# Values of three batches as one split fp32r product, exponentials in mid-batch, scores spaced out

## The chip, the cores and the metric

The kernel runs on one core of one Trainium2 chip. The metric is device microseconds for one execution. The core has five engines with queues of their own: TensorE (PE; PEld is its weight load), VectorE (DVE), ScalarE (ACT), GpSimd (POOL) and SyncE (SP), which here issues every DMA. An instruction waits on semaphores, and what stands behind it on its engine waits with it.

## The reference

Four batches of 12480 tokens with 128 channels go through an attention over 49 agents, and then through a feed-forward network with cosine.

```python
def sm(a, b):                                   # softmax of scaled scores
    s = scale * (a @ b.transpose(0, 2, 1))
    s = s - s.max(-1, keepdims=True)
    e = np.exp(s)
    return e / (e.sum(-1, keepdims=True) + 1e-09)
agent_v = sm(agents, k) @ v                     # per batch: 49 x 128
x = sm(q, agents) @ agent_v                     # 12480 x 128
h = x @ w_in                                    # 128 -> 2048
out = (h * np.cos(h)) @ w_out                   # 2048 -> 128
```

## The kernel before, in words

A batch is cut into 13 groups of 960 tokens, and a group into 8 tiles of 120 tokens. There are two kinds of work.

The main loop (lines 500 to 535) turns weights of the queries into output. It has 832 steps: 4 batches x 13 groups x 16. A step takes two 128-wide slices of the hidden layer and 480 tokens: two matmuls into `ph` (L507; the left side is `a`, which is the agents' values already multiplied by `w_in`, the right side is `pT`), a sine with a quarter-turn of bias on ACT (L510), `(cos - 1) * h` on DVE (L512), and four steps later two matmuls with `w_out` into `one` (L528). The missing `h @ w_out` is added by two matmuls with `b1`, `b2` (L523, L524) at the start of each 480 tokens. Every 8 steps ACT copies `one` to `osb` (L530). `ph` has three buffers in PSUM; `one` has two, and everything else that needs PSUM shares them.

All other work is put between the steps by a plan. `plan(n, f)` runs f behind step n; `extra(n, f)` looks for the next free step of which (n - 4) mod 8 is 1, 3 or 5, so that at most three such pieces stand in 8 steps. A tile scheduler then orders each engine's queue, with this program order as priority, so a piece can come out a few steps earlier or later. The pieces are:

- scores of keys (`scores`, L85): 8 fp32 matmuls, which the hardware profile shows as 16; ACT copies the result to `s` (L163) and DVE keeps a running maximum (L174). `top`, `across` and `spread` make the maximum of all 12480 keys, and `shift` (L202) subtracts it, on POOL in three lots.
- scores of queries (`query`, L85 too): 8 fp32 matmuls, then a maximum and a subtraction on DVE (L334, L341).
- a burst of exponentials: ACT loads another table, runs three exponentials of keys (L206) and those of a set of queries (L345, `pieces`), and loads the table of the sine again. `query_sums` follows on DVE (L349 to L351).
- values (`values`, L224): per group one DMA of v (`vt`, four buffers), 8 fp32 matmuls of 98 columns (the 49 weights twice), shown as 16, and an addition into `av` on DVE (L229). POOL adds up the exponentials for the denominator (`add`, L214); `total` and `inverse` sum them across and take the reciprocal.
- `project` (L255 to L263): four matmuls with `w_in` make the next batch's `a`; `project_out` makes `b1`, `b2`.
- for every group of queries `query_weights` on POOL (L355), `query_turned`: transposes on PE (L364), a copy on ACT (L366), and two casts and two subtractions on POOL (L369, L370) that split the weights into two fp32r parts in `pT`. They are planned 10 and 7 steps ahead of the group's first step.

During batch b's steps the plan prepares batch b + 1: in the order scores of keys, `shift`, scores of queries, burst, values, projection, each as early as `extra` allows. Batch 0 is prepared ahead of the loop, with its values summed in PSUM (`wide`); its own queries 3 to 12 are done in the loop's first 40 steps, with two short bursts.

Of the kernel before, what the change touches and what calls it, by code (L numbers as in the profile page):

```python
# [18 lines left out]
P = 128  # L19
TT = 120  # L20
GT = 8
HT = GT // 2
# [3 lines left out]
EPS = 1e-9  # L26
# [8 lines left out]
HI = 64  # L35
# [5 lines left out]
def agent_attention_cos_ffn(ctx, tc, qT, kT, v, agT, w_in, w_out, outT):  # L41
    nc = tc.nc
    NB, _, N = qT.shape
    NA = agT.shape[2]
    KR = HI + NA
# [6 lines left out]
    NG = N // GRP  # L52
# [8 lines left out]
    make_identity(nc, ident)  # L61
    ones = const.tile([P, 1], F32, name="ones")
    nc.gpsimd.memset(ones, 1.0)
    half_pi = const.tile([P, 1], F32, name="half_pi")
# [32 lines left out]
    class Weights:  # L97
# [45 lines left out]
    class Agents:  # L143
# [72 lines left out]
        def values(self, g):  # L216
            vt = self.sb.tile([TT, GT, P], F32, name="vt", bufs=4)
            nc.sync.dma_start(vt, v[self.b, :, g * GT:(g + 1) * GT, :])
            lone = self.wide is not None
            if g == 0 or not lone:  # L220
                self.po = self.copies(self.wide()[:, 0] if lone else self.psum())
            e, po = self.part(g), self.po
            for t in range(GT):
                nc.tensor.matmul(po, vt[:, t, :], twice(e[:, t, :]), start=(t == 0 and (g == 0 or not lone)),  # L224
                                 stop=(t == GT - 1 and (g == NG - 1 or not lone)))
            if g == (NG - 1 if lone else 0):
                nc.vector.tensor_copy(self.sums, po)
            elif not lone:
                nc.vector.tensor_add(self.sums, self.sums, po)  # L229
# [8 lines left out]
        def inverse(self):  # L238

            pa = self.psum()  # L240
            nc.tensor.matmul(pa[:KR, :1], self.es2, ones[:TT], start=True, stop=True)
            z = self.sb.tile([KR, 1], F32, name="z", bufs=1)
            nc.vector.tensor_scalar_add(z, pa[:KR, :1], EPS)
# [47 lines left out]
    with ExitStack() as pools:  # L291
        sb = pools.enter_context(tc.tile_pool(name="sb", bufs=2))
# [25 lines left out]
        STEP = NCH * NP  # L318
        PER = NG * STEP
        NQ = NB * NG  # L320
        NSTEP = NB * PER
# [59 lines left out]
        if NG == 13:  # L381
            pieces0 = [(0, 1, 2), (3, 4, 5, 6, 7), (8, 9, 10, 11, 12)]
            pieces1 = [(0, 1, 2, 3), (4, 5, 6, 7), (8, 9, 10, 11, 12)]
        pieces = [[tuple(b * NG + g for g in piece) for piece in (pieces1 if b else pieces0)] for b in range(NB)]
        lots = [(0, 4), (4, 4), (8, 5)]


        pre = Plan()
# [4 lines left out]
            pre(3 * c + 2, ws.w_in, c)  # L393
        pre(NG, ab[0].top)
        pre(NG, ab[0].across)
        for n in pieces[0][0]:
            pre(NG, query, n, pieces[0][0], True)
        pre(NG, ab[0].spread)
        for j, (g, n) in enumerate(lots):
            for k in range(g, g + n):  # L400
# [4 lines left out]
        end = 2 * NG + 4  # L405
# [14 lines left out]
        pre(end - 2, query_exp, pieces[0][0])  # L420
        pre(end - 1, query_sums, pieces[0][0])
        pre(end - 1, query_weights, 0)
        pre(end, sine_table)
        pre(end, query_turned, 0)
# [14 lines left out]
        def extra(n, f, *args):  # L439


            while n in taken or (n - LAG) % NP not in (1, 3, 5):
                n += 1
            taken.add(n)
            plan(n, f, *args)
            return n
# [2 lines left out]
            plan(n * STEP - 10, query_weights, n)  # L449
            extra(n * STEP - 7, query_turned, n)  # L450

        def burst(n, todo):
            for f, args in todo:
                plan(n, f, *args)

        t = 0
        for piece in pieces[0][1:]:
            for n in piece:
                t = extra(t, query, n, piece) + 1
            t += 2  # L460
            assert t < piece[0] * STEP - 10
            plan(t, query_exp, piece)
            plan(t + 1, query_sums, piece)
            if piece is pieces[0][1]:
                first = t
        for b in range(1, NB):
            o = (b - 1) * PER
            t = o + (24 if b == 1 else 0)
            for g in range(NG):
                t = extra(t, ab[b].scores, g) + 1  # L470
            t += 2
            plan(t, ab[b].top)
            t = extra(t + 1, ab[b].across)
            t = extra(t + 2, ab[b].spread) + 1
            for g, n in lots:
                plan(t, ab[b].shift, g, n, nc.gpsimd)
            for piece in pieces[b]:
                for n in piece:
                    t = extra(t, query, n, piece) + 1
            t += 2  # L480
            for g, n in lots:
                plan(t, pinned_exp, ab[b], g, n)
            for piece in pieces[b]:
                plan(t, query_exp, piece)
                plan(t + 1, query_sums, piece)
# [10 lines left out]
            assert t < o + PER - 4, (t, o + PER)  # L496


        rs = {}
# [175 lines left out]
```

## Time and profile before

| | |
|---|---|
| median of 3 runs | 1282.7 us (1281.45 to 1284.28) |
| the profiled execution | 1278.94 us, of it 1277.2 us from the first to the last instruction |
| busy: PE, DVE, ACT, POOL | 93%, 85%, 79%, 25% of the span |
| granted TensorE clock | 0.982 on average |

Busy shares are means over stages with different limits. Matmuls overlap, so PE's share says little about how near PE is to its peak; the distance between the starts of two matmuls in the timeline says more. A row of a view with stretches gives the length of a stretch and the busy time of an engine in it.

### The profile page before, as it was taken

What the parts mean: (1) busy time and instruction counts of PE and PEld (TensorE: products, weight loads), DVE (VectorE), ACT (ScalarE), POOL (GpSimd) and SP (SyncE); (2) the same over time, 40 slices, a digit from 0 to 9 for tenths busy, and PEclk for the clock granted to TensorE, in tenths of its full rate; (3) what the DMA queues carried; (4) which work ended last, traced back from release to release, by engine and by line L of the source; (5) the groups of instructions that cost most, each with busy time, mean ns of one, the idle gap of its engine ahead of it and who ended that gap; (6) DMA issues with size and microseconds to landing.
All of it is one profiled execution on the core that took longest, in us unless ns stands there. A gap on an engine that the chain in (4) does not pass through costs nothing.

```text
span 1277.2 us, 17186 instructions
## 1 busy us (share of the span) xinstructions
PE 1186.0 (93%) x6349; PEld 948.7 (74%) x6349; DVE 1087.8 (85%) x1214; ACT 1010.1 (79%) x1115; POOL 313.6 (25%) x341
## 2 busy tenths in 40 slices
PE   8889999996999999969999999997999999999996
PEld 8867787775987887759866787876986666666664
DVE  6878888787789788877899888887789999999997
ACT  2358888667689887677799888667789999999996
POOL 1012113315122124151232223215222212221220
PEclk9999999997999999989999999997999999999999
DMA  9952342332431432414300233322400000000000
GB/s 319 253 165 82 120 125 78 94 108 62 126 91 39 130 96 80 130 55 133 100 32 16 78 109 93 120 67 62 109 16 32 31 32 16 32 31 32 16 32 34
DMA packets 31016, 107.72 MB, mean 84 GB/s; under 512 B 3436, under 2 KB 3820, under 8 KB 30924
## 3 DMA queue, kind: packets, MB, share of 16 engines
q1 hardware_dynamic: 30924, 106.54, 27.2%
q8 instruction: 52, 0.85, 0.3%
q14 instruction: 40, 0.33, 0.1%
HBM read 80.97 MB, written 25.56 MB: 83 GB/s over the span
## 4 chain that ended last, share of the span: by engine, by line
PE 66%; DVE 13%; ACT 12%; issue 5%; DMA 2%; POOL 1%; ACTq 0%; SPq 0%; POOLq 0%; DVEq 0%
PE ph L507 24%; PE one L528 16%; PE one L85 11%; DVE r L512 10%; PE one L224 6%; ACT c L510 6%; ACT osb L530 3%; PE one L523 3%; PE one L364 2%; PE one L524 1%; DMA vt<-v 1%; DVE mx L334 1%; PE ph L93 1%; ACT e L345 1%; PE ph L224 1%
## 5 line engine op out<-in xcount | busy, mean ns | idle before, releaser
L510 ACT ACTIVATE c<-ph,half_pi 128x960 f32<-128x960 f32 x832 | 864.7, 1067 | 194.4 <-PE ph L507 181.1
L512 DVE SCALAR_TENSOR_TENSOR r<-c,ph 128x960 fp32r<-128x960 f32 x832 | 926.1, 1149 | 107.0 <-ACT c L510 97.0
L507 PE MATMUL ph<-pT,a 113*128 113x480 f32 x1664 | 539.4, 405 | 25.0 <-DVE r L512 21.7
L528 PE MATMUL one<-r,w 128*128 128x480 f32 x1664 | 514.5, 389 | 0.7 <-DVE r L512 0.7
L507 PEld LDWEIGHTS ph<-pT,a 113*128 113x128 f32 x1664 | 285.8, 190 | 149.5 <-DVE r L512 89.3
L528 PEld LDWEIGHTS one<-r,w 128*128 128x128 f32 x1664 | 308.8, 190 | 45.7 <-DVE r L512 1.9
L355 POOL TENSOR_TENSOR p<-e,rz 120x392 f32<-120x392 f32 x52 | 44.1, 849 | 779.5 <-PE one L364 677.1
L85 PEld LDWEIGHTS one<-ag,xt 128*120 128x120 f32 x1408 | 165.3, 184 | 19.2 <-ACT osb L530 11.0
L85 PE MATMUL one<-ag,xt 128*120 128x49 f32 x1408 | 163.8, 264 | 2.6 <-ACT osb L530 1.7
L370 POOL TENSOR_TENSOR pT<-p,pT 49x480 fp32r<-49x480 f32 x104 | 126.8, 1219 | 8.0
L224 PE MATMUL one<-s,vt 120*128 120x98 f32 x624 | 81.3, 285 | 26.6 <-ACT osb L530 26.6
L224 PEld LDWEIGHTS one<-s,vt 120*128 120x128 f32 x624 | 81.6, 205 | 30.3 <-ACT osb L530 27.9
L369 POOL CAST pT<-p 49x480 fp32r<-49x480 f32 x104 | 61.1, 587 | 57.2 <-ACT p L366 52.3
L530 ACT COPY osb<-one 128x480 f32<-128x480 f32 x104 | 57.9, 557 | 2.1 <-PE one L528 2.1
L523 PE MATMUL one<-pT,b 113*128 113x480 f32 x104 | 46.1, 443 | 12.0 <-ACT osb L530 6.7
L334 DVE TENSOR_REDUCE mx<-one 120x8 f32<-120x392 f32 x49 | 27.6, 563 | 29.0 <-PE one L85 28.9
L523 PEld LDWEIGHTS one<-pT,b 113*128 113x128 f32 x104 | 19.5, 187 | 35.5 <-issue 12.5
L364 PE MATMUL one<-ident,p 120*113 120x120 f32 x208 | 37.2, 279 | 5.4 <-ACT s L163 1.8
L364 PEld LDWEIGHTS one<-ident,p 120*113 120x113 f32 x208 | 28.4, 176 | 18.3 <-ACT osb L530 11.3
L524 PE MATMUL one<-pT,b 113*128 113x480 f32 x104 | 39.6, 381 | 0.0
L202 POOL TENSOR_TENSOR s<-s,mxb 120x1568 f32<-120x1568 f32 (+1 forms) x9 | 31.4, 3518 | 27.2 <-DVE mxb L198 27.2
L349 DVE TENSOR_REDUCE rz<-e 120x32 f32<-120x1568 f32 (+2 forms) x12 | 22.7, 1916 | 17.2 <-ACT e L345 17.2
(91 smaller groups left out, 506.2 us busy)
## 6 DMA issues: line engine op xcount, KB each, us to landing
xt<-qT SPq DMA_DIRECT2D x52, 480.0 KB, 3.4
vt<-v SPq DMA_DIRECT2D x52, 480.0 KB, 4.3
outT<-osb SPq DMA_DIRECT2D x51, 480.0 KB, 2.5
xt<-kT SPq DMA_DIRECT2D x46, 480.0 KB, 3.4
c<-kT SPq DMA_DIRECT2D x6, 480.0 KB, 6.1
raw<-w_in SPq DMA_DIRECT2D x4, 512.0 KB, 6.1
raw<-w_out SPq DMA_DIRECT2D x4, 512.0 KB, 10.2
outT<-osb SPq DMA_DIRECT2D x2, 240.0 KB, 2.0
```

The source lines that it names most:

```text
L85: nc.tensor.matmul(ps[:, t, :], xt[:, t * TT:(t + 1) * TT], ag[:, b, :], start=True, stop=True)
L224: nc.tensor.matmul(po, vt[:, t, :], twice(e[:, t, :]), start=(t == 0 and (g == 0 or not lone)), stop=(t == GT - 1 and (g == NG - 1 or not ...
L364: nc.tensor.transpose(pt[:KR, t * TT:(t + 1) * TT], p_in[n % 2][:, t, :KR], ident[:TT, :TT])
L369: nc.gpsimd.tensor_copy(pT[own, c], p[own])
L370: nc.gpsimd.tensor_sub(pT[other, c], p[own], pT[own, c].bitcast(F32))
L507: nc.tensor.matmul(ph[:, j, :CH], ai[:, f], pTs[q % 3][:, c], start=True, stop=True)
L510: nc.scalar.activation(cos, h, AF.Sin, bias=half_pi, scale=1.0)
L512: nc.vector.scalar_tensor_tensor(r, cos, 1.0, h, op0=ALU.subtract, op1=ALU.mult)
L523: nc.tensor.matmul(po, b1[k], pTs[q % 3][:, c], start=True, stop=False)
L524: nc.tensor.matmul(po, b2[k], pTs[q % 3][:, c], start=False, stop=False)
L528: nc.tensor.matmul(po, w1[:, f, :], r[:, j, :], start=False, stop=(f == NF - 1))
L530: nc.scalar.copy(osb[:, c * CH:(c + 1) * CH], po)
```

## The change

For batches 1 to 3 the values are made another way. GpSimd rounds each v tile to fp32r and takes the remainder, so that the two parts and two columns of ones stand side by side in `v12` (258 columns); it does the same with the exponentials in `e12` (98 columns). One fp32r matmul for each tile multiplies all parts with all parts, and the columns of ones give the denominators. This is done in two halves of four tiles, each with two buffers (`v12` shares those of `raw`). DVE adds the 98 x 258 result up in `o`. `folded` adds the parts together with three small matmuls by a constant matrix `fold`, and replaces `total` and `inverse`; `add` is no longer called in these batches.

The plan changes too. Queries are scored in other sets: 3 to 7 at the start, then 8 to 19 during batch 0, 20 to 32 during batch 1, 33 to 45 during batch 2, and 46 to 51 during batch 3. Scores of keys and queries alternate, and `spread_out` spaces them. The burst has a fixed place: behind step 112 of batch 0, and behind step 98 of the others. The values follow it, one group in five steps at the earliest. Ahead of the burst stand `top`, `across`, `spread` and `shift`. There is one short burst less at the start and one more in batch 3.

```diff
+    fold = const.tile([2 * NA, KR], F32, name="fold")     # + memset and four affine_selects on gpsimd
...
-            raw = self.sb.tile([P, 512, 2], U32, name="raw", bufs=2)
+            raw = self.sb.tile([P, 516, 2], U32, name="raw", bufs=2)[:, :512]
...
     class Fast(Agents):
+        def values(self, g):
+            if self.wide is not None:
+                return super().values(g)
+            sb = self.sb
+            W = 2 * P + 2
+            vt = sb.tile([TT, GT, P], F32, name="vt", bufs=4)
+            nc.sync.dma_start(vt, v[self.b, :, g * GT:(g + 1) * GT, :])
+            if g == 0:
+                self.o = sb.tile([2 * NA, W], F32, name="o", bufs=1)
+            e, po = self.part(g), self.psum()[:2 * NA, :W]
+            for h in range(2):
+                ts = slice(h * HT, (h + 1) * HT)
+                v12 = sb.tile([TT, HT, W], F32R, name="raw", bufs=2)
+                e12 = sb.tile([TT, HT, 2 * NA], F32R, name="e12", bufs=2)
+                nc.gpsimd.memset(v12[:, :, 2 * P:].bitcast(F32), 1.0)
+                for x12, x, w in ((v12, vt[:, ts, :], P), (e12, e[:, ts, :], NA)):
+                    nc.gpsimd.tensor_copy(x12[:, :, :w], x)
+                    nc.gpsimd.tensor_sub(x12[:, :, w:2 * w], x, x12[:, :, :w].bitcast(F32))
+                for t in range(HT):
+                    nc.tensor.matmul(po, e12[:, t], v12[:, t], start=(h == t == 0), stop=(h == 1 and t == HT - 1))
+            if g == 0:
+                nc.vector.tensor_copy(self.o, po)
+            else:
+                nc.vector.tensor_add(self.o, self.o, po)
+
+        def folded(self):
+            pa = self.psum()
+            for x in range(2):
+                nc.tensor.matmul(pa[:, :KR], self.o[:, x * P:(x + 1) * P], fold, start=(x == 0), stop=(x == 1))
+            nc.tensor.matmul(pa[:KR, 256:257], fold, self.o[:, 2 * P:2 * P + 1], start=True, stop=True)
+            nc.vector.tensor_copy(self.av, pa[:, :KR])
+            self.inverse_of(pa[:KR, 256:257])
...
+        BURST = [112] + [98] * (NB - 1)
+        early = [(3, 4, 5, 6, 7)]
+        pieces, n = [], 8
+        for b in range(1, NB + 1):
+            upto = min(b * NG + 7, NQ)
+            k = upto - n
+            cuts = [n + k * i // 3 for i in range(4)]
+            pieces.append([tuple(range(x, y)) for x, y in zip(cuts, cuts[1:]) if y > x])
+            n = upto
...
+        def spread_out(todo, t, end):
+            for i, lot in enumerate(todo):
+                t = extra(t, *lot) + 1
+                if i + 1 < len(todo):
+                    t += max(0, (end - t) // (len(todo) - i - 1) - 1)
+            return t
+        def burst(t, end, group):
+            for piece in group:
+                plan(t, query_exp, piece)
+                plan(t + 1, query_sums, piece)
...
         for b in range(1, NB):
             o = (b - 1) * PER
-            t = o + (24 if b == 1 else 0)
-            for g in range(NG):
-                t = extra(t, ab[b].scores, g) + 1
-            t += 2
+            at = o + BURST[b - 1]
+            both = ...                       # scores of keys and of queries, alternating
+            last = spread_out(both, t, at - 18)
+            t = last + 1
             plan(t, ab[b].top)
             t = extra(t + 1, ab[b].across)
             t = extra(t + 2, ab[b].spread) + 1
             for g, n in lots:
                 plan(t, ab[b].shift, g, n, nc.gpsimd)
-            for piece in pieces[b]:
-                for n in piece:
-                    t = extra(t, query, n, piece) + 1
-            t += 2
             for g, n in lots:
-                plan(t, pinned_exp, ab[b], g, n)
-            for piece in pieces[b]:
-                plan(t, query_exp, piece)
-                plan(t + 1, query_sums, piece)
+                plan(at, pinned_exp, ab[b], g, n)
+            burst(at, o + PER, group)
+            t = at + 1
             for g in range(NG):
-                plan(t, ab[b].add, g)
-                t = extra(t, ab[b].values, g) + 1
-            plan(t, ab[b].total)
-            t = extra(t + 1, ab[b].inverse) + 1
+                t = max(extra(t, ab[b].values, g) + 1, at + 1 + 5 * (g + 1))
+            t = extra(t + 1, ab[b].folded) + 1
...
+        at = (NB - 1) * PER + BURST[NB - 1]
+        assert spread_out(scored(pieces[NB - 1]), t, at - 4) < at
+        burst(at, NSTEP, pieces[NB - 1])
```

More of the change, by code (lines that the diff above doesn't have):

```diff
@@ L61, in agent_attention_cos_ffn @@
     make_identity(nc, ident)
+    fold = const.tile([2 * NA, KR], F32, name="fold")
+    nc.gpsimd.memset(fold, 0.0)
+    for part in (fold[:, :NA], fold[:, HI:]):
+        for base in (0, -NA):
+            nc.gpsimd.affine_select(out=part, in_=part, compare_op=ALU.not_equal, fill=1.0,
+                                    base=base, pattern=[[-1, NA]], channel_multiplier=1)
     ones = const.tile([P, 1], F32, name="ones")
@@ L241, in inverse, with inverse_of @@
             nc.tensor.matmul(pa[:KR, :1], self.es2, ones[:TT], start=True, stop=True)
+            self.inverse_of(pa[:KR, :1])
+        def inverse_of(self, sums):
             z = self.sb.tile([KR, 1], F32, name="z", bufs=1)
-            nc.vector.tensor_scalar_add(z, pa[:KR, :1], EPS)
+            nc.vector.tensor_scalar_add(z, sums, EPS)
             self.rz = self.sb.tile([KR, 1], F32, name="rz", bufs=1)
@@ L380, in agent_attention_cos_ffn @@
         ab = [Fast(sb, small, b, None if b else pair) for b in range(NB)]
[L381 to L384, printed above, removed]
+        assert NG == 13
+        BURST = [112] + [98] * (NB - 1)
[7 more added lines that the diff above has]
+            n = upto
         lots = [(0, 4), (4, 4), (8, 5)]
+        first = (0, 1, 2)
         pre = Plan()
@@ L395, in agent_attention_cos_ffn @@
         pre(NG, ab[0].across)
-        for n in pieces[0][0]:
-            pre(NG, query, n, pieces[0][0], True)
+        for n in first:
+            pre(NG, query, n, first, True)
         pre(NG, ab[0].spread)
@@ L419, in agent_attention_cos_ffn @@
             pre(NG + 5 + 3 * c, w_product, c)
-        pre(end - 2, query_exp, pieces[0][0])
-        pre(end - 1, query_sums, pieces[0][0])
+        pre(end - 2, query_exp, first)
+        pre(end - 1, query_sums, first)
         pre(end - 1, query_weights, 0)
@@ L450, in agent_attention_cos_ffn, with scored @@
             extra(n * STEP - 7, query_turned, n)
[L452 to L457, printed above, removed]
-            for n in piece:
-                t = extra(t, query, n, piece) + 1
-            t += 2
-            assert t < piece[0] * STEP - 10
-            plan(t, query_exp, piece)
-            plan(t + 1, query_sums, piece)
-            if piece is pieces[0][1]:
-                first = t
+        def spread_out(todo, t, end):
[6 more added lines that the diff above has]
+            for piece in group:
+                assert t + 4 < piece[0] * STEP - 2 and t < end
+                plan(t, query_exp, piece)
+                plan(t + 1, query_sums, piece)
+        def scored(group):
+            return [(query, n, piece) for piece in group for n in piece]
+        t = spread_out(scored(early), 0, 0) + 2
+        burst(t, 3 * STEP, [early[0]])
         for b in range(1, NB):
             o = (b - 1) * PER
-            t = o + (24 if b == 1 else 0)
-            for g in range(NG):
-                t = extra(t, ab[b].scores, g) + 1
-            t += 2
+            at = o + BURST[b - 1]
+            group = pieces[b - 1]
+            qs, ks = scored(group), [(ab[b].scores, g) for g in range(NG)]
+            both = []
+            while qs or ks:
+                both += ks[:1] + qs[:1]
+                ks, qs = ks[1:], qs[1:]
+            last = spread_out(both, t, at - 18)
+            t = last + 1
             plan(t, ab[b].top)
@@ L476, in agent_attention_cos_ffn @@
                 plan(t, ab[b].shift, g, n, nc.gpsimd)
-            for piece in pieces[b]:
-                for n in piece:
-                    t = extra(t, query, n, piece) + 1
-            t += 2
+            assert t <= at, (t, at)
             for g, n in lots:
-                plan(t, pinned_exp, ab[b], g, n)
-            for piece in pieces[b]:
-                plan(t, query_exp, piece)
-                plan(t + 1, query_sums, piece)
+                plan(at, pinned_exp, ab[b], g, n)
+            burst(at, o + PER, group)
+            t = at + 1
             for g in range(NG):
-                plan(t, ab[b].add, g)
-                t = extra(t, ab[b].values, g) + 1
-            plan(t, ab[b].total)
-            t = extra(t + 1, ab[b].inverse) + 1
+                t = max(extra(t, ab[b].values, g) + 1, at + 1 + 5 * (g + 1))
+            t = extra(t + 1, ab[b].folded) + 1
             i = b % 2
@@ L495, in agent_attention_cos_ffn @@
             plan(t, ab[b].judge)
-            assert t < o + PER - 4, (t, o + PER)
+            t += 1
+            assert t < o + PER - 3, (t, o + PER)
+        at = (NB - 1) * PER + BURST[NB - 1]
+        assert spread_out(scored(pieces[NB - 1]), t, at - 4) < at
+        burst(at, NSTEP, pieces[NB - 1])
         rs = {}
```

## The prediction

> **What bounds the kernel now.** First the page's busy shares.
>
> ```profile
> span 1277.2 us, 17186 instructions
> PE 1186.0 (93%) x6349; PEld 948.7 (74%) x6349; DVE 1087.8 (85%) x1214; ACT 1010.1 (79%) x1115; POOL 313.6 (25%) x341
> ```
>
> Three engines are near their limit and POOL has room, on average. A mean hides stages, so second the stretches: the four periods of 208 steps, with DVE's L512, one for each step.
>
> ```profile
> core 0: us, DVE busy (x), PEclk, DMA share, GB/s
> 81.10:410.20 329.10, 231.80 (x207) 0.98 0.31 94
> 410.20:718.50 308.30, 231.28 (x207) 0.98 0.27 82
> 718.50:1026.60 308.10, 231.15 (x207) 0.98 0.24 72
> 1026.60:1268.00 241.40, 231.84 (x212) 1.00 0.07 28
> ```
>
> Third, the same view of the second period's stages, and the steps of the last one that have nothing beside them.
>
> ```profile
> 410.20:471.30 61.10, 45.39 (x40) 1.00 0.38 117
> 471.30:481.50 10.20, 8.95 (x9) 1.00 0.07 28
> 481.50:548.30 66.80, 45.11 (x41) 1.00 0.37 111
> 548.30:573.40 25.10, 7.85 (x7) 0.80 0.15 40
> 573.40:632.50 59.10, 44.35 (x41) 1.00 0.44 126
> 632.50:653.40 20.90, 17.81 (x17) 1.00 0.06 24
> 653.40:708.60 55.20, 52.92 (x49) 1.00 0.07 27
> 708.60:718.50 9.90, 8.89 (x8) 1.00 0.07 10
> 1026.60:1246.90 220.30, 211.25 (x193) 1.00 0.07 28
> ```
>
> The bare step is 220.3 / 192 = 1.148 us, and DVE is busy 211.25 of 220.3 us there: DVE sets it. 208 steps make 238.8 us, so the periods cost 90.3, 69.5, 69.3 and 2.6 us above the floor, 231.7 in all. A change can only win from these. By stage (the cuts lie at steps 0, 40, 48, 88, 96, 136, 152, 200): scores of keys 61.1 - 45.9 = 15.2; maximum 1.0; scores of queries 20.9; burst 15.9; values 13.2; projection 2.5; bare steps 0.1; one group of keys alone in 8 steps 0.7.
>
> ```profile
> 410.20:471.30 61.10, 22.88 (x192) 23.16 (x192) 1.00 0.38 117
> 481.50:548.30 66.80, 21.85 (x192) 22.01 (x192) 1.00 0.37 111
> ```
> ```profile
> 573.40:632.50 59.10, 22.28 (x186) 22.20 (x185) 1.00 0.44 126
> ```
>
> (The same stretches with L85 alone, then with L224.) At 16 matmuls a group that is 12 groups of keys at 1.27 us, 12 of queries at 1.74 us, and 11.6 of values at 1.14 us. The missing group of queries and 1.4 of values lie in the burst's stretch; without them the burst costs 15.9 - 3.3 = 12.6.
>
> **The change, part by part.**
>
> *Values on PE and DVE.* The timeline of PE, and a group of DVE:
>
> ```profile
> 605.46 1.92 PE L224 MATMUL one<-s,vt 120*128 120x98 f32 x16
> 607.16 0.68 PE L528 MATMUL one<-r,w 128*128 128x480 f32 x2
> 607.68 0.60 PE L507 MATMUL ph<-pT,a 113*128 113x480 f32 x2
> 608.12 0.60 PE L528 MATMUL one<-r,w 128*128 128x480 f32 x2
> ```
> ```profile
> L229 DVE TENSOR_TENSOR av<-av,one 128x98 f32<-128x98 f32 x36 | 9.0, 251 | 0.7 <-PE one L224 0.7
> ```
>
> Sixteen take 607.16 - 605.46 = 1.70 us. An fp32r matmul of 480 columns takes 0.44 / 2 = 0.22; one of 258 no less than 258/480 of it, 0.12, and eight 0.95. A step needs four of 0.22 on PE, so 1.148 leaves 0.27 idle, and five steps 1.35: the new group fits, the old did not. DVE adds 98 x 258 in place of 128 x 98; its floor is the limit there, so this shows: about 0.4 us, estimated from 251 ns for 98 columns. I take 0.5 us a group, under the 0.7 of the lone group of keys. If nothing else held them, twelve groups (the first falls into the burst) would cost 6.0 a batch where thirteen cost 14.8.
>
> *Values on POOL.* Rows of its timeline, and one group:
>
> ```profile
> 472.80 1.26 POOL L369 CAST pT<-p 49x480 fp32r<-49x480 f32 x2 [0.31 <-ACT p L366]
> 474.14 2.51 POOL L370 TENSOR_TENSOR pT<-p,pT 49x480 fp32r<-49x480 f32 x2
> 482.86 10.47 POOL L202 TENSOR_TENSOR s<-s,mxb 120x1568 f32<-120x1568 f32 x3 [6.21 <-DVE mxb L198]
> 499.92 0.85 POOL L355 TENSOR_TENSOR p<-e,rz 120x392 f32<-120x392 f32 x1 [6.59 <-PE one L364]
> ```
> ```profile
> 555.20 0.51 POOL L212 COPY es<-s 120x392 f32<-120x392 f32 x1 [0.79 <-ACT s L206]
> ...
> 560.63 11.99 POOL L214 TENSOR_TENSOR es<-es,s 120x392 f32<-120x392 f32 x11
> ```
> ```profile
> L158 POOL MEMSET av<- 128x15 f32 x4 | 0.4, 112 | 1.5 <-PE one L268 1.4
> ```
>
> Half a group is a memset (0.11), a cast of 512 (0.63 x 512/480 = 0.67), a subtraction of 512 (1.25 x 512/480 = 1.33), a cast of 196 (0.35, between half of 0.51 and all of it) and a subtraction of 196 (0.6, a little over half of 1.09): 3.1 us, 6.2 a group. The low end goes by the lots of L202, 10.47 us for 5096 elements: 708 x (2.05 + 1.22 ns) + 0.11 = 2.4, 4.85 a group. I take 6.2, because L370 has the same operands and types. For each group of queries POOL also needs 0.85 + 3.85 = 4.7 us. The removed `add` (13 x 1.09) lay beside the burst and comes back as nothing.
>
> So POOL is the new limit. From the burst to the last values (62 steps, floor 71.2 us) it owes 12 x 6.2 + 4 x 4.7 + 2 (until PE frees the first buffer) = 95.2 us. What is behind its queue? The main loop's `pT`. The fourth group of queries after the burst is needed 64 steps after it in the first period and 62 in the next two (73.5 and 71.2 us); ahead of its `pT` stand 10 groups of values and 4 sets: 62 + 18.8 + 2 = 82.8, so the loop loses at least 9.3 to 11.6 a batch. Values that are later still have room: the projection ends at step 197, 389 and 597, and 208, 416 and 624 need it. Pieces do come out later than planned where the scheduler sees a resource busy, and I assume that it puts the product behind further steps while POOL works. The 6.0 lie inside that for the most part. I take 12 a batch, 36 in all, against 3 x 14.8 = 44.4: -8.4.
>
> The rule that speaks for the change is the Trainium skill's, GPSIMD Engine Reference, section "Elementwise — side-by-side cycle accounting": about 2.6 cycles an element with two inputs and 1.03 at best with one, at 1.2 GHz. By it half a group is an estimated 708 x (2.17 + 0.86 ns) = 2.1 us and POOL keeps up, as in the second rival; L370's 2.61 ns an element in sequence speaks against it.
>
> SP issues as many DMAs of `vt` as before; a buffer now comes free when POOL has read it, and four of them lie three groups ahead.
>
> *Scores.* By the new plan's step numbers 50 of the 88 groups still stand five in 16 steps, 8 four, and 30 three or fewer. Before: 39 x 1.27 + 49 x 1.74 = 134.8. After: 50 x 1.5 (the mean) + 8 x 1.4 + 30 x 1.05 (toward the 0.7 of a lone one) = 118: -16. Bounds: 0, and -35 if loose ones cost 0.7 and mixing saves 0.1.
>
> *Bursts.* ACT in the second one:
>
> ```profile
> 552.32 1.28 ACT L206 ACT_TABLE_LOAD   x1
> 553.62 1.52 ACT L206 ACTIVATE s<-s 120x1568 f32<-120x1568 f32 x1
> ...
> 558.62 4.62 ACT L345 ACTIVATE e<-e 120x1568 f32<-120x1568 f32 x3
> 563.25 1.28 ACT L510 ACT_TABLE_LOAD   x1
> ```
> ```profile
> L345 ACT ACTIVATE e<-e 120x1960 f32<-120x1960 f32 x5 | 9.2, 1830 | 0.0
> ```
>
> It holds ACT from 552.32 to 564.53. Before, L202's 10.47 us ran 42 steps ahead of it. Now `shift` stands at step 112 with the burst at 112, 304 with 306, and 504 with 514. Where they meet, the last exponential of keys waits for the last lot: 10.47 + 1.83 + what queries need, 4.6, + 1.28 = 18.2 instead of 12.2, and an estimated 0.7 until the maximum is through PE and DVE: +6.7. With two steps' lead (2.3 us) +4.4, with ten nothing. All of ACT's queue stands behind, sines first, and PE and DVE run dry. +11.1; bounds 0 (the maximum comes earlier) and 15. The short bursts: one of 1.28 + 1.83 + 1.28 = 4.4 goes, one of three small exponentials, two table loads and an estimated 3 x 0.84 (half of the 1.52 for 1568 elements, and a little) make 5.1, comes: +0.7.
>
> *Rest.* `folded` for `total` and `inverse`, and the constants at the start: nothing; PE, DVE and POOL wait in those places already, and uncovered they are under 2 us.
>
> **Sum:** -16 + 11.1 + 0.7 - 8.4 = -12.6. The profiled execution's 1278.94 (1277.2 and 1.7 around it) becomes 1266; it stands 3.8 below the median of 1282.7, so the median becomes **1270 us**.
>
> **Rivals.** For the first, the 62 steps behind the second burst, with the five engines' columns:
>
> ```profile
> 564.50:653.40 88.90, 86.80 (x479) 74.19 (x480) 73.98 (x89) 67.39 (x78) 23.55 (x28) 0.95 0.33 95
> ```
>
> 1. *Slower: PE waits for POOL in order.* If the scheduler takes POOL's work for shorter than it is, PE's queue holds the products at their planned steps, and each main step waits behind. Groups two steps apart (at 157 and 159, 173 and 175) then stall PE some 4 us each. The window lasts 95.2 and about 5 in which POOL waits for PE: 28 above the floor, 84 in all: +39.6 in the place of -8.4, **1318 us**. It decides from 16 us a batch, a window of 87. For it: 95.2 is more than the 88.9 us that 62 such steps, projection included, took before; against it: pieces drift already. I give 0.30.
> 2. *Faster: POOL keeps up.* At 4.85 a group its debt is 79 us, and 71.2 + 6.0 + 1.5 (an estimate for the slow clock behind the burst, the granted 0.80 above) = 78.7 is what the others need. Values cost 7.5 a batch, 22.5 in all: **1257 us**. 0.17.
> 3. *The scores are not spread:* the 50 dense groups set the price and all cost the same as before. **1286 us**. 0.10.
>
> **How the numbers follow.** The forecast has 0.43, with a range of its own of 1260 to 1282. Under 0.2% (2.6 us) this kernel's runs can't be told apart. Faster: 0.36 of the forecast and rival 2, 0.53. The same: 0.03 and half of rival 3, 0.08. Slower: 0.04, rival 1 and half of rival 3, 0.39. 1250 to 1318 leaves half of rival 1 above and 0.05 below.
>
> **What the profile after would show.** POOL's busy time near 500 us, with subtractions of 512 at 1.3 us; four products of 258 columns in place of eight of 98 for each half, under 0.13 us apart. If ACT's L206 waits for POOL's `s` in two bursts, +11.1 is right. If PE's products wait for POOL by several us each, rival 1 holds; if L507 waits for POOL's `pT` instead, the forecast. Periods: 322, 310, 300 and 248 us. It would be wrong above all if a subtraction of 512 took under 1.1 or over 1.5 us, or if one period grew to 330.

## The result, and the profile after

The changed kernel takes **1327.2 us** (median of four runs, 1322.9 to 1331.7), the kernel before 1282.5 beside it (1281.5 to 1284.3): a ratio of 1.034, with an interval of 1.031 to 1.037. The forecast was 1270, and its range ended at 1318. The profiled execution is the longest of the four, 1331.7 us.

First the page's span and busy shares:

```profile
span 1329.9 us, 16919 instructions
...
PE 1182.6 (89%) x6049; PEld 943.2 (71%) x6049; DVE 1097.2 (83%) x1217; ACT 1017.3 (76%) x1117; POOL 475.9 (36%) x694
```

POOL gained 162 us of work and is still idle two thirds of the time; nothing in this row says that it is the trouble. The four periods of 208 steps, with DVE's L576 (L512 before):

```profile
80.90:415.40 334.50, 231.97 (x206) 0.94 0.30 86
415.40:745.80 330.40, 234.79 (x209) 0.94 0.28 83
745.80:1068.20 322.40, 233.26 (x209) 0.95 0.22 67
1068.20:1321.00 252.80, 229.61 (x209) 0.99 0.08 30
```

They were 329.1, 308.3, 308.1 and 241.4 us. The first grew by 5, the second by 22, the third by 14, the last by 11, and the granted clock of the first three fell from 0.98 to 0.94 and 0.95. Next the 64 steps behind each burst's 16, which hold the values and the projection (columns: PE, PEld, DVE, ACT, POOL busy, then PEclk):

```profile
309.50:394.20 84.70, 78.66 (x384) 62.56 (x383) 76.88 (x81) 73.22 (x80) 71.23 (x122) 1.00 0.35 88
603.40:700.80 97.40, 85.17 (x390) 67.94 (x389) 77.18 (x81) 73.35 (x80) 76.98 (x134) 0.93 0.30 82
928.70:1027.40 98.70, 86.00 (x392) 68.08 (x390) 77.35 (x82) 73.47 (x80) 74.17 (x129) 0.93 0.19 56
```

Sixty-four bare steps are 73.5 us, so these stretches lie 11.2, 23.9 and 25.2 above the floor. In the two long ones no engine is busy the whole time: PE 85 and 86 of 97 and 99 us, POOL 77 and 74. That is the sign of two engines that wait for each other in turn. POOL's timeline in the second stretch shows it:

```profile
618.33 0.10 POOL L277 MEMSET raw<- 120x8 f32 x1
...
620.91 0.10 POOL L277 MEMSET raw<- 120x8 f32 x1
...
623.51 0.86 POOL L401 TENSOR_TENSOR p<-e,rz 120x392 f32<-120x392 f32 x1
624.29 1.23 POOL L415 CAST pT<-p 49x480 fp32r<-49x480 f32 x2
625.60 2.51 POOL L416 TENSOR_TENSOR pT<-p,pT 49x480 fp32r<-49x480 f32 x2
628.06 0.10 POOL L277 MEMSET raw<- 120x8 f32 x1
...
637.91 0.57 POOL L280 TENSOR_TENSOR e<-s,e 120x196 fp32r<-120x196 f32 x1
643.25 0.11 POOL L277 MEMSET raw<- 120x8 f32 x1 [4.77 <-PE one L282]
```

and PE's beside it:

```profile
623.95 0.64 PE L282 MATMUL one<-raw,e 120*98 120x258 f32 x4
624.43 0.59 PE L571 MATMUL ph<-pT,a 113*128 113x480 f32 x2
...
627.98 0.61 PE L571 MATMUL ph<-pT,a 113*128 113x480 f32 x2
630.85 0.72 PE L282 MATMUL one<-raw,e 120*98 120x258 f32 x4 [2.26 <-POOL e L280]
633.40 1.18 PE L282 MATMUL one<-raw,e 120*98 120x258 f32 x4 [1.83 <-POOL raw L277]
...
634.77 1.00 PE L571 MATMUL ph<-pT,a 113*128 113x480 f32 x2
```

A set of `pT` (623.51 to 628.06) stands on POOL ahead of a split. PE meets that group's products at 628.6, stands 2.26 us for the first half and 1.83 for the second, and the main steps stand behind it. Behind that its matmuls take 1.00 us a pair in place of 0.60 (634.77 against 624.43): the granted clock is lower there. Now POOL is ahead, but there are two half-group buffers, and at 638.5 both are full: it stands 4.77 us until PE, with slower matmuls and late main steps, has read one. The list of waits has both directions:

```profile
POOL raw L277 <- PE one L282: 26.6, 15, 4.8
...
PE one L282 <- POOL e L280: 22.7, 8, 7.7
...
PE one L282 <- POOL raw L277: 18.4, 14, 1.8
```

(The columns are the sum in us, the number of waits and the longest.) Two of the eight waits on L280, of 7.7 and 7.2 us, lie in bursts, at a batch's first group. The other 7.8 us and the 18.4 us on L277 are PE's waits for the split of the later groups, 26.2 us in all.

For the experiments, each kernel is split into those three stretches and the rest of its main loop, in us above 1.148 a step, from its own profiled execution. The numbers of before are the prediction's: three times its 13.2 + 2.5 of the second period, and 231.7 in all. (Cut at the starts of before's own steps, the two would be 51 and 181.)

| kernel | values and projection | rest | sum |
|---|---|---|---|
| before | 47 | 185 | 232 |
| after | 60.4 | 224.1 | 284.5 |
| new plan, old values | 33.3 | 220.3 | 253.6 |
| after, no split | 20.2 | 213.3 | 233.5 |
| after, dense scores | 60.4 | 209.3 | 269.7 |
| the same, early subtraction | 62.4 | 198.1 | 260.5 |
| the same, three buffers | 36.9 | 198.7 | 235.6 |
| after, three buffers | 36.9 | 214.9 | 251.8 |

The profiled execution is not always near the median: the rows "after" and "dense scores" show the longest execution of their kernel, "no split" and "after, three buffers" the shortest. Of the 52 us by which the loop grew from before to after, 13 lie in the values' stretches and 39 in the rest. So the values are not the whole loss, and not the larger part of what separates the two kernels.

### The profile page after: what moved, and what is told of

The parts are those of the page before. It is cut to its first block, busy times and chain, and to the rows that moved or that the text cites. A ratio compares the mean times of both kernels' runs of the same rounds, so it can differ in the third digit from the quotient of the medians.

```text
span 1329.9 us, 16919 instructions
## 1 busy us (share of the span) xinstructions
PE 1182.6 (89%) x6049; PEld 943.2 (71%) x6049; DVE 1097.2 (83%) x1217; ACT 1017.3 (76%) x1117; POOL 475.9 (36%) x694
## 3 DMA queue, kind: packets, MB, share of 16 engines
q1 hardware_dynamic: 30924, 106.54, 26.6%
## 4 chain that ended last, share of the span: by engine, by line
PE 53%; POOL 15%; DVE 13%; ACT 10%; issue 5%; DMA 3%; SPq 0%; ACTq 0%; POOLq 0%
PE ph L571 18%; PE one L592 14%; PE one L92 11%; DVE r L576 10%; ACT c L574 6%; POOL raw L280 4%; ACT osb L594 2%; PE one L587 2%; POOL s L209 2%; DMA vt<-v 2%; POOL raw L279 2%; POOL e L280 2%; PE one L282 2%; POOL pT L416 2%; PE one L410 2%
## 5 line engine op out<-in xcount | busy, mean ns | idle before, releaser
L576 DVE SCALAR_TENSOR_TENSOR r<-c,ph 128x960 fp32r<-128x960 f32 x832 | 931.2, 1150 | 136.8 <-ACT c L574 128.3
L571 PE MATMUL ph<-pT,a 113*128 113x480 f32 x1664 | 545.1, 409 | 24.3 <-DVE r L576 21.4
L592 PE MATMUL one<-r,w 128*128 128x480 f32 x1664 | 524.3, 398 | 0.7 <-DVE r L576 0.7
L571 PEld LDWEIGHTS ph<-pT,a 113*128 113x128 f32 x1664 | 296.9, 195 | 131.9 <-DVE r L576 78.3
L592 PEld LDWEIGHTS one<-r,w 128*128 128x128 f32 x1664 | 320.7, 196 | 51.2 <-issue 2.2
L282 PE MATMUL one<-raw,e 120*98 120x258 f32 x312 | 57.8, 309 | 54.4 <-POOL e L280 22.7
L282 PEld LDWEIGHTS one<-raw,e 120*98 120x98 f32 x312 | 45.4, 179 | 69.5 <-POOL e L280 26.4
L280 POOL TENSOR_TENSOR raw<-vt,raw 120x512 fp32r<-120x512 f32 x78 | 93.3, 1198 | 0.0
L587 PE MATMUL one<-pT,b 113*128 113x480 f32 x104 | 48.2, 464 | 27.3 <-ACT osb L594 11.3
L587 PEld LDWEIGHTS one<-pT,b 113*128 113x128 f32 x104 | 20.2, 195 | 52.1 <-ACT osb L594 17.3
L279 POOL CAST raw<-vt 120x512 fp32r<-120x512 f32 x78 | 48.0, 616 | 0.8
L280 POOL TENSOR_TENSOR e<-s,e 120x196 fp32r<-120x196 f32 x78 | 44.6, 574 | 0.0
```

What stands on the lines that cost most here:

```text
L279: nc.gpsimd.tensor_copy(x12[:, :, :w], x)
L280: nc.gpsimd.tensor_sub(x12[:, :, w:2 * w], x, x12[:, :, :w].bitcast(F32))
L282: nc.tensor.matmul(po, e12[:, t], v12[:, t], start=(h == t == 0), stop=(h == 1 and t == HT - 1))
L571: nc.tensor.matmul(ph[:, j, :CH], ai[:, f], pTs[q % 3][:, c], start=True, stop=True)
L576: nc.vector.scalar_tensor_tensor(r, cos, 1.0, h, op0=ALU.subtract, op1=ALU.mult)
L587: nc.tensor.matmul(po, b1[k], pTs[q % 3][:, c], start=True, stop=False)
```

## The experiments

**The plan alone, and the values alone.** The changed kernel with the `values`, `add`, `total` and `inverse` of before:

```
-            t = extra(t + 1, ab[b].folded) + 1
+            plan(t, ab[b].total)
+            t = extra(t + 1, ab[b].inverse) + 1
...          (and `add` planned beside each `values`; class Fast without its own values)
```

> The new plan with the old values (fp32, 8 matmuls a group, add, total and inverse), nothing else. Theory P (the main loop waits for POOL's split): most of the +45 us hang on the split, so this stands at 1275 to 1295 us. Theory S (the plan itself costs: scores that alternate and stand apart cost about 1.7 us a group instead of 1.4, some +25 us for 88 groups, and the burst that waits for the shift and the late burst some +15 more): 1315 to 1335 us.

Measured: 1299.6 us, 1.011 of before (1.009 to 1.013), between the ranges of the two theories. The other half, the old plan with the new `values`:

```
-                plan(t, ab[b].add, g)
                 t = extra(t, ab[b].values, g) + 1
-            plan(t, ab[b].total)
-            t = extra(t + 1, ab[b].inverse) + 1
+            t = extra(t + 1, ab[b].folded) + 1
```

> The old plan with the new values (split on POOL, fp32r, folded), which then stand three in 8 steps. Theory P: POOL owes 12 x 5.4 + 2.5 x 4.7 = 77 us for stretches that took 59 us, so about +18 us a batch, 1320 to 1345 us, with PE waiting for raw and e. Theory S: the product itself is harmless or a gain, 1260 to 1290 us.

Measured: 1321.8 us, 1.030 (1.028 to 1.032). Each part is slower by itself, 14 and 38 us, and together they cost 44. With the new plan, the new values add 0.023, some 30 us, to the old ones. The plan does help old values: in the same three stretches it leaves

```profile
sum 253.70, PE 253.56 PEld 216.82 DVE 223.27 ACT 210.19 POOL 55.29; mean PE 84.52 PEld 72.28 DVE 74.42 ACT 70.06 POOL 18.43
```

33.3 above the floor with 32 groups in them, where the old plan had 47 with some 35. PE is busy in 253.6 of the 253.7 us: one limit, and no waiting in turn.

**No split.**

```
-                v12 = sb.tile(...); e12 = sb.tile(...); (memset, two casts, two subtractions)
+                if g == 0:
+                    v12 = ...; (the same)
+                    self.parts = (self.parts if h else []) + [(v12, e12)]
+                v12, e12 = self.parts[h]
```

> The new kernel, but POOL splits only the first group of each batch and all 13 groups' products use those parts (the other groups' v and exponentials are left out of the result): same matmuls, same plan, 36 of 39 splits gone from POOL. Theory P: PE's waits for raw and e (about 20 us on PE in each of the value stretches of batches 2 and 3) and the late pT go, 1280 to 1300 us. Theory S: at most 15 us are won, 1312 us or more.

This kernel leaves out the values of twelve groups in thirteen: their products read the split of the first group again. The values went over `FAST_MAX`, the limit above which the kernel computes everything again on a general path behind the main loop (8787 us), so its time says nothing. The same kernel with that limit out of reach:

> The changed kernel in which POOL splits only the first group of values of batches 1 to 3 and the products of the other twelve groups read that same split (so twelve thirteenths of the values are left out, and with them the test that sends large values to the general path). Products, copies of vt and all else stay. Theory P: the split's share of the cost goes, 1327 to 1285 or less, with value stretches at 0.3 to 0.5 us a group above the floor. Theory S: the values hardly count, 1315 to 1325.

Measured: 1292.6 us, 1.007 (1.004 to 1.010): 35 us of the change's 44 are gone, though the products and DVE's additions are all there. The DMAs of `vt` are there too, but nothing reads them, so they run early: the last is issued at 186.6 us, and in the three stretches the DMA moves 25 or 26 GB/s where it moved 56 to 88. The three stretches:

```profile
sum 240.60, PE 234.15 PEld 190.03 DVE 228.51 ACT 219.85 POOL 64.16; mean PE 78.05 PEld 63.34 DVE 76.17 ACT 73.28 POOL 21.39
```

20.2 above the floor, 7.5 of it projection (three times 2.5): 12.7 over the 32 groups in them, 0.4 us a group on PE and DVE. So the cost hangs on the split, or on the loads that left the stretches with it; and if on the split, this run does not say whether by POOL's time or by the waiting. The next runs keep both the split and the loads in place.

**Three buffers.** The changed kernel with one size changed (the loads of the weights ahead of the loop share `raw`, so theirs changes too):

```
-            raw = self.sb.tile([P, 516, 2], U32, name="raw", bufs=2)[:, :512]
+            raw = self.sb.tile([P, 516, 2], U32, name="raw", bufs=3)[:, :512]
...
-                v12 = sb.tile([TT, HT, W], F32R, name="raw", bufs=2)
-                e12 = sb.tile([TT, HT, 2 * NA], F32R, name="e12", bufs=2)
+                v12 = sb.tile([TT, HT, W], F32R, name="raw", bufs=3)
+                e12 = sb.tile([TT, HT, 2 * NA], F32R, name="e12", bufs=3)
```

> The changed kernel with three half-group buffers for the split in place of two. Theory P (PE's queue waits for POOL's split, and POOL then waits for PE to give a buffer back, 26.6 us in 15 waits in the changed kernel's trace): a third buffer lets POOL run half a group ahead, so at most those 26.6 us come back, and as the split still owes 5.15 us a group and stands behind the pT set, about half: 1327 goes to 1310 to 1318. If PE's wait is only POOL's throughput and order (a group is planned every 5 steps, 5.75 us, and pT takes 4.7 more in 16 steps), under 5 us come back: 1322 to 1327. Theory S (the plan costs, not the split): no change, 1325 to 1329.

Measured: 1300.7 us, 1.016 (1.010 to 1.021): 26.5 us below the changed kernel. That is more than the half of POOL's 26.6 us of waiting which I expected to come back. POOL does the same work (476.5 us against 475.9). The two waits at the buffers, and the three stretches:

```profile
POOL raw L277 <- PE one L282: 8.5, 4, 3.4
PE one L282 <- POOL raw L277: 7.2, 6, 2.8
```
```profile
298.70:378.60 79.90, 77.50 (x383) 62.43 (x383) 76.28 (x81) 73.14 (x80) 70.10 (x120) 1.00 0.35 93
585.20:673.40 88.20, 81.87 (x392) 65.72 (x390) 76.60 (x81) 73.34 (x80) 76.18 (x132) 0.96 0.35 90
899.80:989.00 89.20, 82.04 (x391) 65.33 (x391) 76.98 (x82) 73.50 (x80) 71.63 (x124) 0.96 0.22 62
```

POOL's wait is 18 us shorter, PE's wait for the later groups' split 19 (7.2 in place of 26.2; on L280 only the two of the bursts are left). Each stretch is 5 to 10 us shorter, and in the last two the granted clock is 0.96 where it was 0.93. These are the shortest execution of this kernel and the longest of the changed one, 37 us apart and not 26.5; and the clock moved along with the waits, so this run alone does not separate the two.

**Dense scores.** The new plan with keys and then queries at five groups in 16 steps, as before, in the place of keys and queries by turns with even gaps:

```
-            both = [] ... (one of keys, one of queries)
-            last = spread_out(both, t, at - 18)
+            last = spread_out(ks + qs, max(t, at - 18 - 78), 0)
```

> The new kernel with the scores as before: all keys first, then the queries, as close together as the slots allow, ending about where they end now; burst, shift and values unchanged. Theory S: the scores fall back to 1.4 us a group and the halved clock in the stretches of scores goes, 1297 to 1308 us. Theory P: no more than 8 us from the new kernel, 1318 to 1330 us.

Measured: 1313.6 us, 1.023 (1.021 to 1.024), 14 below the changed kernel and between the ranges of the two theories. The scores and bursts of the three batches (changed kernel, then this one):

```profile
sum 665.70, PE 587.84 PEld 484.24 DVE 534.79 ACT 502.67 POOL 180.88; mean PE 195.95 PEld 161.41 DVE 178.26 ACT 167.56 POOL 60.29
```
```profile
sum 650.30, PE 585.21 PEld 477.81 DVE 531.95 ACT 505.60 POOL 180.72; mean PE 195.07 PEld 159.27 DVE 177.32 ACT 168.53 POOL 60.24
```

With the scores spread these stretches are 15.4 us longer with the same work in them. Where spreading was to win 16, it loses about as much against dense scores. (The granted clock differs too: 0.91, 0.93 and 0.96 with the scores spread, 0.93, 0.95 and 0.95 with them dense.)

**Early subtraction.** Dense scores, and the maximum and POOL's subtraction right behind the keys, some 42 steps ahead of the burst:

```
+            t = spread_out(ks, max(t, at - 18 - 78), 0) + 1
             plan(t, ab[b].top) ... shift
+            t = spread_out(qs, t, 0)
```

> As the run with dense scores (keys, then queries, 1313.6 us), but the maximum and the subtraction of it (POOL, three lots) stand right after the keys and the queries after them, some 42 steps ahead of the burst. If the exponentials' wait for POOL (1.4 + 2.4 us in each of two bursts) and the pT set behind the subtraction (7 us of PE in the third period) cost what the trace shows, 8 to 13 us come back: 1300 to 1306. If those waits only take the place of others: 1311 to 1316.

Measured: 1307.4 us, 1.018 (1.015 to 1.022), 1.4 above what was expected. Against the run before it that is 0.004, or 5.5 us, and the two intervals overlap. The trace is clearer: in the changed kernel ACT's second burst has two holes, in this one none. (The dense run has the same two, 1.37 and 2.44 us, in its second and third burst.)

```profile
573.45 1.51 ACT L213 ACTIVATE s<-s 120x1568 f32<-120x1568 f32 x1
576.33 1.51 ACT L213 ACTIVATE s<-s 120x1568 f32<-120x1568 f32 x1 [1.38 <-POOL s L209]
580.28 1.84 ACT L213 ACTIVATE s<-s 120x1960 f32<-120x1960 f32 x1 [2.43 <-POOL s L209]
```
```profile
563.73 4.64 ACT L213 ACTIVATE s<-s 120x1568 f32<-120x1568 f32 x3
```

**Early subtraction and three buffers.** The two theories left were that two buffers make PE and POOL wait in turn (R), and that the third had helped only through the clock (T). The edit is that of the three buffers, on the run above.

> The run with the early subtraction (1307.4 us, 1.018 of before) and a third half-group buffer. Theory R (the ring of two buffers is what makes PE and POOL wait for each other in turn): the value stretches go from 4.2 to 7.7 us above the floor in 16 steps to the 0.9 to 3 that three buffers gave with the new plan, 22 to 27 us in all: 1280 to 1286, no slower than before. Theory T (the third buffer helped only with spaced scores, through the clock): under 10 us: 1298 to 1306.

Measured: 1279.4 us, 0.997 of before (0.995 to 0.999): 28 us below the same kernel with two buffers. The three stretches with two and with three:

```profile
sum 282.80, PE 250.37 PEld 198.82 DVE 230.93 ACT 219.65 POOL 224.22; mean PE 83.46 PEld 66.27 DVE 76.98 ACT 73.22 POOL 74.74
```
```profile
sum 257.30, PE 240.87 PEld 193.13 DVE 229.53 ACT 219.37 POOL 218.57; mean PE 80.29 PEld 64.38 DVE 76.51 ACT 73.12 POOL 72.86
```

The stretches are 25.5 us shorter, and the rest of the loop stays (198.1 and 198.7). (The loop also starts 4.7 us earlier in this execution. Its start lies anywhere from 76.5 to 84.0 us in the kernels here, with two buffers and with three.) PE's busy time in them fell by 9.5 us, which is the clock (0.98, 0.93 and 0.95 before, 1.00, 0.98 and 0.96 now), and its idle time by 16. T needed spaced scores and falls; R holds, and the clock is part of what the waits cost. A third half-group of buffer gives back the larger half of the 44 us, because it turns the values' stretches from 15 us above the 47 of before to 10 below.

**The split handed over a group ahead.** `values` in two parts, the split planned at the step of the product before it, five steps ahead of its own:

```
+                t = extra(at + 2 + 5 * (g + 1), ab[b].product, g)
+                if g + 1 < NG:
+                    plan(t, ab[b].values, g + 1)
```

> The run with early subtraction and three buffers, with the split of each group handed to POOL five steps (5.75 us) ahead of its product on PE. If what is left above the floor with three buffers (6.5 us in 16 steps of the second and third batch's values, where the pT set stands ahead of a split) is PE's queue holding a product too near to its split: 5 to 10 us below the run with three buffers. If a product that waits for the whole group and not for half of it keeps the buffers longer, POOL stands still for them instead: the same, or up to 8 us more.

Measured: 1284.3 us, 1.000 (0.9985 to 1.0016); nothing won, and perhaps 4 us lost. The reason expected for that, POOL standing still for buffers, is not what the trace shows: in the second stretch POOL waits 1.8 us for PE, and 1.6 without the handing over. POOL's own time would explain it; from 588.9 to 633.5 us it works without a gap. A group is 5.15 us of it (below), a set of `pT` 4.55 (623.51 to 628.06 above), and sixteen steps five apart hold 3.2 groups and one set, 21.0 us, where 16 bare steps last 18.4. Six steps apart they hold 2.67 groups: 18.3. This plan has no room for that: in the first period the last piece would stand at step 210 of 208.

**Old plan, looser values.** The old bursts leave batches 2 and 3 room for a group every six steps. Batch 1 has none, and keeps the old values, one group every four steps; the split is a group ahead, with three buffers:

```
+            if self.b < 2:
+                return super().values(g)
...
+                    t = max(extra(t, ab[b].values, g) + 1, at + 4 * (g + 1))        # batch 1
...
+                    t = extra(at + 1 + 6 * (g + 1), ab[b].product, g)               # batches 2, 3
+                    if g + 1 < NG:
+                        plan(t, ab[b].values, g + 1)
```

> The kernel before with its own plan, in which batch 1 keeps the fp32 values, one group every 4 steps in place of every 3, and batches 2 and 3 have the new product, one group every 6 steps, split on POOL a group ahead with three buffers. The old values cost 13.2 us above the floor a batch. Theory R: the new ones cost 4 or less where POOL is ahead, and spaced old ones 0.87 a group in place of 1.14: 1282 - 18 - 3.5 = 1258 to 1266. If POOL's split makes the main loop wait even then (pT behind it): 1270 to 1285.

Measured: **1255.7 us**, 0.979 of before (0.975 to 0.982), the fastest kernel here. Eighty steps behind each burst of batches 2 and 3, with twelve groups and nothing of the projection in them:

```profile
569.00:664.90 95.90, 92.40 (x460) 75.29 (x459) 91.92 (x94) 88.57 (x96) 84.17 (x144) 1.00 0.30 88
866.20:962.00 95.80, 92.30 (x459) 75.18 (x458) 91.97 (x94) 88.60 (x96) 79.31 (x135) 1.00 0.22 68
```

Eighty bare steps are 91.8: 4.1 above, at a full clock, with POOL busy 84 of 96 us. In the changed kernel 64 such steps with eleven groups and the projection cost 24, and the projection took 2.5 of its own in the kernel before.

**Old plan, looser old values.** How much of that is the spacing? Only the fp32 values of before, spaced by four and seven steps:

```
-                t = extra(t, ab[b].values, g) + 1
+                t = max(extra(t, ab[b].values, g) + 1, at + (4 if b == 1 else 7) * (g + 1))
```

> The kernel before with only its fp32 values spaced, one group every 4 steps in batch 1 and every 7 in batches 2 and 3, where they stood every 3. Spaced values cost 0.87 us a group in the run of the new plan alone against 1.14 here: 39 groups x 0.27 = 10 us, 1270 to 1276. If spacing gives nothing by itself (DVE and PE lose as much to each lone group): 1280 to 1285.

Measured: 1275.2 us, 0.994 (0.991 to 0.996), as expected. So 8 us are the spacing's, and some 20 the new product's in 26 groups (spaced by six steps and not seven).

**Two buffers there too.** The kernel of 1255.7 us with

```
-                v12 = sb.tile([TT, HT, W], F32R, name="raw", bufs=3)
-                e12 = sb.tile([TT, HT, 2 * NA], F32R, name="e12", bufs=3)
+                v12 = sb.tile([TT, HT, W], F32R, name="raw", bufs=2)
+                e12 = sb.tile([TT, HT, 2 * NA], F32R, name="e12", bufs=2)
```

> The run of the old plan with batches 2 and 3 on spaced new products split a group ahead (1255.7 us, 0.9785 of before), with two half-group buffers in place of three. Theory R, strong form (two buffers hold POOL up wherever they stand): POOL cannot split ahead while the products of the group before are pending, every group has POOL idle for PE's product and the value stretches rise from about 1 to over 3 us in 16 steps: 1270 to 1285. Theory R, weak form (two buffers hurt only where groups stand so close that POOL has no time to lose; six steps are 6.9 us, a split 5.15): within 4 us, 1254 to 1260.

Measured: 1263.0 us, 0.986 (0.983 to 0.989): 7 us, between the two forms of R. The same two stretches:

```profile
572.80:672.20 99.40, 93.33 (x460) 75.73 (x459) 91.80 (x93) 88.17 (x95) 84.83 (x146) 0.99 0.30 85
874.10:973.10 99.00, 93.20 (x460) 75.44 (x459) 91.72 (x93) 88.11 (x95) 81.80 (x140) 1.00 0.22 65
```

7.6 and 7.2 above the floor for 4.1 and 4.0. Two buffers cost something even with room between the groups, 7 us in 26 of them, and far more where POOL has no time to lose, 28 in 39.

## Why the prediction was wrong

Two terms of the sum failed. The values were to win 8.4 us, and by the table their stretches cost 13 more. The scores, bursts and the rest were to win 4.2, and cost 39 more; most of that distance is the scores' -16. (Their own sum, 134.8 - 118, is nearer -17.)

**Values on POOL: the price was too high, and the time came out too low.** Groups of POOL's instructions by shape:

```profile
L280 POOL TENSOR_TENSOR raw<-vt,raw 120x512 fp32r<-120x512 f32 x78 | 93.3, 1198 | 0.0
...
L279 POOL CAST raw<-vt 120x512 fp32r<-120x512 f32 x78 | 48.0, 616 | 0.8
L280 POOL TENSOR_TENSOR e<-s,e 120x196 fp32r<-120x196 f32 x78 | 44.6, 574 | 0.0
...
L279 POOL CAST e<-s 120x196 fp32r<-120x196 f32 x78 | 27.4, 354 | 8.2 <-ACT s L213 8.2
...
L277 POOL MEMSET raw<- 120x8 f32 x78 | 8.4, 108 | 90.0 <-DVE wf L124 63.2 <-PE one L282 26.6
```

The five add up to 2.85 us, and one half-group follows the other by 2.58 (618.33 to 620.91, the two memsets in the timeline), because each starts some 0.05 before the record of the one ahead of it ends. So a group is some 5.15 us; the forecast had 6.2 and as its low end 4.85, and the subtraction of 512 took 1.20 and not 1.3. With 5.15 the prediction's own sum up to the fourth `pT` is 10 x 5.15 + 4 x 4.7 + 2 = 72.3, and the steps up to it take 71.2 to 73.5. By that sum POOL should have just kept up, nearly as in the second rival (over the whole window 82.6 for POOL, 78.7 for the others). The failing step is the "2 (until PE frees the first buffer)": it was counted once, and a wait of this kind came 15 times, 26.6 us in all. Two half-group buffers used in turn (a ring) leave POOL 2.58 us of lead, less than the 4.55 of one `pT` set ahead of a split. With it failed "I assume that it puts the product behind further steps while POOL works": PE stands at the products, 26.2 us in all, and the main steps stand behind them. Rival 1 had this mechanism, and its 28 us a batch are close to the 23.9 and 25.2 of the second and third, projection included. What it lacked is the other direction: it gave POOL's waiting 5 us a batch in a sentence, and the prediction never asked what a third buffer would do. "Pieces drift already", the argument against rival 1, fell with the same rows. The three runs with a third buffer show what was in its place: 26.5, 28 and 7 us came back with POOL's work unchanged. The forecast's 12 a batch fit the first batch alone (11.2, projection and all); why that one is spared, no run here tells.

What the Trainium skill's GPSIMD Engine Reference, section "Elementwise — side-by-side cycle accounting", gave as an estimate, 2.1 us a half-group, is below the 2.58 measured; L370's price for the same operands, 3.1, is about as far above it.

**Values on PE and DVE.** Right as far as the runs show. Four products start within 0.48 us (623.95 to 624.43), 0.12 each, and DVE's addition takes 0.42; the run without split, with its loads elsewhere, makes it 0.4 us a group where I took 0.5.

**Scores.** The step that failed is the price of a loose group, 1.05 "(toward the 0.7 of a lone one)". By the starts of every sixteenth step in the changed kernel's trace, four groups in 16 steps cost 6.2 us above the floor (1.55 each), two and a quarter 3.1 (1.4), and the six late queries 12.6 (2.1 each). In all, the sixteens with scores cost 152 us for 86 groups, with a short burst and some slow clock in them, where the prediction had 118 for 88 and 134.8 before. A group that stands alone does not get cheaper. The sixteen steps from 1146.9 hold one query: they take 20.7 us with DVE busy 18.4, and bare ones 18.4 with DVE busy 17.6. So DVE, the engine at its floor, has 0.8 us more to do and 1.5 more idle, part of it while PE does the scores, part behind a wait of PE for `pT`. The term should have been zero, as in rival 3, or above; the dense run puts the spread scores, with what they do to the bursts, at +15.

**Bursts.** The waits of ACT for POOL's `s` are there in two bursts, 1.38 + 2.43 us each, where 6.7 and 4.4 were forecast. The third, forecast at zero, has its cost elsewhere: POOL's subtraction stands ahead of a `pT` that PE needs.

```profile
881.79 10.48 POOL L209 TENSOR_TENSOR s<-s,mxb 120x1568 f32<-120x1568 f32 x3 [17.44 <-DVE mxb L205]
...
893.52 2.46 POOL L416 TENSOR_TENSOR pT<-p,pT 49x480 fp32r<-49x480 f32 x2
```
```profile
894.77 0.77 PE L587 MATMUL one<-pT,b 113*128 113x480 f32 x1 [6.95 <-POOL pT L416]
```

The prediction asked who waits for `shift` itself, and not what stands behind it in POOL's queue. 3.8 + 3.8 + 7 is 14.6 in the trace against 11.1 forecast, and moving the subtraction back gave 5.5. The first burst has one more wait that was in no term:

```profile
296.35 1.14 PE L410 MATMUL one<-ident,p 120*113 120x120 f32 x4 [7.37 <-POOL p L401]
```

PE stands until POOL has made `p`, the weights of a query group whose exponentials are in that very burst; POOL first splits values, until 293.3 us, and then waits 2.13 us for DVE's sums of these exponentials. No run here takes that wait out by itself.

**Periods.** 322, 310, 300 and 248 us were forecast, 334, 330, 322 and 253 came. That "one period grew to 330" was named as a sign that the forecast is wrong above all; two reached it. The clock was in no term of the sum, and it is part of each period: 0.94 to 0.99 was granted, and 0.98 to 1.00 before. Behind the waits shown above PE's matmuls ran slower, so the stretch after such a wait pays again.

## What to carry to other kernels

Where one engine prepares and an in-order engine consumes inside a loop, add up the producer's time per stretch of the loop, with all that shares its queue, and compare its lead with the longest other piece of work in that queue: here one buffer's 2.58 us against 4.55. A mean busy share of 36% hides a ring that is one buffer short. Then space the work so that this sum fits. An even spread of small pieces is no gain by itself when each piece adds the same instructions to the engine at its floor.

## What the hardware showed

The granted clock drops in this kernel without a long wait ahead of it. The same steps, 256 to 272, with the same work, in the changed kernel and with three buffers:

```profile
488.60:517.50 28.90, 27.93 (x140) 24.08 (x140) 20.49 (x23) 18.12 (x22) 4.42 (x5) 0.82 0.32 97
```
```profile
473.00:497.60 24.60, 23.41 (x139) 20.00 (x139) 20.40 (x23) 17.98 (x22) 4.43 (x5) 1.00 0.38 112
```

4.3 us for one drop. PE's timeline of the changed kernel shows where it begins and ends:

```profile
493.08 1.88 PE L92 MATMUL one<-ag,xt 128*120 128x49 f32 x16 [0.79 <-ACT osb L594]
...
495.78 1.00 PE L571 MATMUL ph<-pT,a 113*128 113x480 f32 x2
...
505.64 0.60 PE L571 MATMUL ph<-pT,a 113*128 113x480 f32 x2
```

Half the clock for the 9.9 us between the last two rows would give 0.83 over the 28.9, and 0.82 was granted. The Trainium skill's TensorE: Matmul & The Clock Gate, section "Part 1: The HAM clock gate (the "warmup" mystery)", has the clock halve after an idle window of about 3.4 us; here the longest idle in the seven us ahead of it is 0.79, so the row disagrees with the sentence as it stands. What sets it off was not tried. In the changed kernel it falls into bursts (0.76 granted from 267.6 to 309.5 us), stretches of scores (0.82 in the row above) and the values' waits (0.93), and it differs between executions of like kernels.
